# The second layer of a gated feed-forward kernel turned over: 26 products of weight block sums, read back from DRAM, with gated block sums of 512 tokens

## The chip, the core and the metric

The kernel runs on one core of one Trainium2 chip. A core has a matrix engine (TensorE; PE in the profile, with its weight loads as PEld), three engines for elementwise work (VectorE is DVE, ScalarE is ACT, GpSimd is POOL) and SyncE (SP), which here only starts DMA transfers. SBUF is the on-chip memory of 128 partitions, PSUM the small memory that TensorE writes its products to, DRAM the memory off the core. Each engine works through its own queue in order; an instruction that waits holds everything behind it in that queue. The metric is the time of one execution on the device in microseconds (us), lower is better. The kernel before has a median of 660.98 us in three runs (660.61 to 662.32).

## The reference

Two blocks follow each other. A retention block turns q, k and v (4 batches, 8 heads, 768 steps, 64 numbers each) into 3072 rows of 512, with a decaying state per head. A feed-forward block multiplies these rows by W_in, gates the result and multiplies by W_out:

```python
for t in range(S):
    state = gamma[None, :, None, None] * state + np.einsum('bhd,bhe->bhde', k[:, :, t], v[:, :, t])
    y[:, :, t] = scale * np.einsum('bhd,bhde->bhe', q[:, :, t], state)
x = y.transpose(0, 2, 1, 3).reshape(3072, 512)
h = x @ w_in                      # (512, 2048)
sp = np.maximum(h, 0.0) + np.log1p(np.exp(-np.abs(h)))
g = h * erf(sp)
return (g @ w_out).astype(np.float32)     # w_out (2048, 512)
```

Everything is computed in 32-bit floats. The two weights arrive as 8-byte floats, and the kernel takes them apart and rebuilds them as 4-byte floats on VectorE and ScalarE while they are loaded.

## The kernel before

Tokens come in pieces of 128, numbered j (24 of them). The first 512 tokens (j = 0 to 3) go through an opening stage, with their hidden values in four groups g = 0 to 3 of 512 and plain products; this stage also loads and converts the weights and ends at about 132 us. All later tokens go through a loop over g = 4 to 23 (`for g in range(G0 + 1, NG)`, with g = 4 written out ahead of it). Two successive g are the two halves, s = 0 and 1, of the 2048 hidden values of one chunk of 256 tokens.

The first layer of a g (`hidden_steps`, line 987) replaces 32 block products by the 26 of a fast scheme, in the table `STEPS`. Each step is one product of a sum of W_in blocks with a sum of x blocks, 128 columns wide and two matmuls long. The W_in sums are made once (`sum_in`, line 385), the 18 x sums per chunk (`x_sums`, line 969). A step's result lies in one of four PSUM banks (tiles `hp` and `r`), and is copied by ScalarE or added by VectorE (line 999, 18 additions a g) into up to two blocks of h. The bank is free for its next step only then.

After the last step come Softplus (line 859) and Erf (line 866) on ScalarE, and two multiplications by h on VectorE (`gated`, line 885).

The second layer (`project_part`, line 1070) uses the seven products of a 2 by 2 fast scheme (`PRODUCTS`) for each g: four matmuls of 128 x 128 by 256 columns each, the gated block held still and W_out (with its four sums T1 to T4) streamed, all from SBUF. Four gated sums a g come from VectorE (`g_sums`, line 1052). Three products of g - 1 are spread among the steps of g, four stand in a row at the end of g. The finished chunk is put together by VectorE (`put_part`) and written in two DMAs of 256 KB.

At the end of each g lies a visit of the recurrence (`sub_visit`): scores, state and values of the next 128 tokens in small matmuls of 64 x 64, masks (line 677), additions to the state (lines 819 and 839) and to the rows (line 834). `prepared` scales and transposes the next pieces of q and k on VectorE (five instructions a piece). `load(j)` starts the DMAs of a piece three ahead: one for k (line 208), 32 small ones of 16 KB for blocks of q and k (line 190, from `load_blocks`), one for v (line 218). All of them, and the writes of the output, are issued by SP.

The order of the work is written by hand: every engine gets its instructions in the order of the Python statements.

Of the kernel before, what the change touches and what calls it, by code (L numbers as in the profile page):

```python
# [25 lines left out]
FG = 4  # L26
# [9 lines left out]
OUT = {"11": 0, "12": 1, "21": 2, "22": 3, "T3": 1, "T1": 4, "T2": 5, "T4": 6}  # L36

PRODUCTS = {
    1: ("11", "11"), 2: ("12", "21"), 3: ("S4", "22"), 4: ("22", "T4"),
    5: ("S1", "T1"), 6: ("S2", "T2"), 7: ("S3", "T3"),  # L40
}

N_W, N_X = 26, 18
W_SUMS = (
# [83 lines left out]

OP = {"+": ALU.add, "-": ALU.subtract}
# [5 lines left out]
def kernel(  # L140
# [31 lines left out]
    act = ctx.enter_context(tc.tile_pool(name="act", bufs=2))  # L172
# [4 lines left out]


# [16 lines left out]
    def load(j):  # L195
        b, c = divmod(j, NC)
        if j == JPC - 1:

            x = act.tile([P, N], F32, name="e", bufs=1)
            KQ[j] = x[:, : 2 * d_model].rearrange("p (i h d) -> p i h d", i=2, h=H)  # L200
            V[j] = x[:, 2 * d_model : 3 * d_model].rearrange("p (h d) -> p h d", h=H)
        else:
            KQ[j] = loads.tile([P, 2, H, D], F32, name="kq")
            V[j] = loads.tile([P, H, D], F32, name="v")
# [21 lines left out]
    w_out_sb = const.tile([P, 2, 7, FG, DH], F32, name="w_out_sb")  # L226
# [5 lines left out]
    def w_out_of(ft):  # L232
        half, s, i = ft // (2 * FG), ft % (2 * FG) // FG, ft % FG
        return w_out_sb[:, s, 2 * half : 2 * half + 2, i, :]
# [4 lines left out]
    spare = [w_out_sb[:, s, 4:7].rearrange("p a b c -> p (a b c)") for s in range(2)]  # L239
# [4 lines left out]
    LO = slice(2 * CE + 2, 2 * CE + 2 + CE // 2)  # L244
    whole_powers = [later[:, i * CE : (i + 1) * CE].bitcast(U32) for i in range(2)]
    powers = [
        [x.bitcast(U16) for x in two] for two in (
            (spare[0][:, LO], spare[1][:, LO]),
            (later[:, : CE // 2], later[:, CE // 2 : CE]),
            (spare[1][:, : CE // 2], spare[1][:, CE // 2 : CE]),  # L250
        )
# [18 lines left out]
    def load_piece(n, *parts):  # L270
# [16 lines left out]
        else:  # L287
            for d in range(2):
                nc.sync.dma_start(
                    w.rearrange("p (d f c) -> p d f c", d=2, f=2)[:, d],  # L290
                    x[i * 2 * P : (i + 1) * 2 * P, d * words * DH : (d + 1) * words * DH].rearrange(
                        "(f p) c -> p f c", p=P
                    ),
                )

    def load_pieces_after(n):
        for later in range(n + 1, n_p):
            if place[later] == place[n]:
                load_piece(later)
                break  # L300

    def whole_conversion(n):
# [6 lines left out]
        for part, rows in parts:  # L309
            last = n > 0 or rows.start == 1  # L310
            words = spare[place[n]][:, : 2 * CE].bitcast(U32)
            if which == "in":
                f = slice(2 * P) if part is None else slice(part * P, (part + 1) * P)
                fb = 2 * half + at
                to = w_in_sb[:, s, 4 * fb : 4 * fb + 4, f].rearrange("p (h k) f -> p h k f", h=2)
            else:
                to = w_out_sb[:, s, 2 * half : 2 * half + 2, at * 2 : at * 2 + 2, :]
            words = words.rearrange("p (h a b w) -> p h a b w", h=2, a=2, w=2)
            power = whole_powers[n % 2].rearrange(
                "p (h q a b) -> p q h a b", q=1 if part is None else 2, h=2, a=2  # L320
# [28 lines left out]
    def shifted_conversion(n):  # L349
# [3 lines left out]
        words = spare[place[n]].bitcast(U32)[:, : 2 * CE].rearrange("p (h a b w) -> p h a b w", h=2, a=2, w=2)  # L353
        top = spare[place[n]].bitcast(U16)[:, 4 : 4 + 4 * CE].rearrange(
            "p (h a b w) -> p h a b w", h=2, a=2, w=4
# [4 lines left out]
        else:  # L360
            to = w_out_sb[:, s, 2 * half : 2 * half + 2, at * 2 : at * 2 + 2, :]
        up, down = (
            x.rearrange("p (h a b) -> p h a b", h=2, a=2) for x in powers[2 if n == n_p - 1 else n % 2]
# [24 lines left out]
    def sums(s):  # L388

        assert ("project", s) in done  # L390
        x = {name: w_out_sb[:, s, at] for name, at in OUT.items()}
        for to, a, b in (("T1", "12", "11"), ("T2", "22", "T1"), ("T3", "22", "12"), ("T4", "21", "T2")):
            nc.scalar.activation(x[to], x[b], AF.Copy, scale=-1.0)
            nc.gpsimd.dma_start(x[to], x[a], accum_op=ALU.add)
            done.add((to, s))
            yield

# [14 lines left out]
    def later_sums():  # L412
        for s in range(2):
            yield from sums(s)

    weight_steps = weights()
    last_steps = later_sums()
# [9 lines left out]
    def need(*what):  # L427
        nonlocal room
        while what not in done:
            cost = next(weight_steps, None)  # L430
            if cost is None:
                next(last_steps)
            room -= cost or 0
# [4 lines left out]
    ident = const.tile([P, P], F32, name="ident")  # L438
# [18 lines left out]
    causal = const.tile([P, C], F32, name="causal")  # L457
# [17 lines left out]
    adds_of = {JPC: range(2), JPC + 1: range(1), JPC + 2: range(1)}  # L475
    assert (JPC + 2) % NC == 0 and NC > 1

# [25 lines left out]
    kq_b = const.tile([P, NC, 2, HP, 4], F32, name="kq_b")  # L503
    by_b = const.tile([P, 2, HP], F32, name="by_b")

    def load_block_scales(g):
        nc.gpsimd.tensor_copy(idle_out, HS[g][:, N - 1 :])
        for s, d in itertools.product(range(2), range(2)):
            part = slice((2 * s + d) * 32, (2 * s + d + 1) * 32)
            for u in range(HP):  # L510
                nc.gpsimd.dma_start(
                    kq_b[part, 0, 0, u],
# [4 lines left out]
    def block_scales():  # L517
        nc.vector.reciprocal(by_b[:, 0], by_b[:, 1])
        nc.vector.reciprocal(kq_b[:, 0, 1], kq_b[:, 0, 0])
        nc.vector.tensor_scalar(kq_b[:, 0, 1], kq_b[:, 0, 1], unscale, None, op0=ALU.mult)  # L520
        for c in range(1, NC):
            nc.gpsimd.tensor_tensor(
                kq_b[:, c], kq_b[:, c - 1], by_b[:, :, :, None].to_broadcast([P, 2, HP, 4]),
                op=ALU.mult,
# [50 lines left out]
    def prepared(j):  # L575

        if j >= NJ:
            return
        nc.vector.tensor_tensor(
            KQ[j][:, 0], KQ[j][:, 0],  # L580
            kq_s[:, j % NC, 0, :, None].to_broadcast([P, H, D]), op=ALU.mult,
        )
        yield
        blocks = (KB[j], KQ[j][:, 1].rearrange("p h d -> p (h d)"))
        for i, x in enumerate(blocks):
            x = x.rearrange("p (u a d) -> p u a d", u=HP, d=32)
# [801 lines left out]
```

## Time and profile before

| what | value |
|---|---|
| median of three runs | 660.98 us (660.61 to 662.32) |
| span of the profiled execution, first to last instruction | 659.9 us |
| PE busy | 654.1 us, 99% |
| DVE, ACT, POOL busy | 504.4, 289.6 and 21.5 us |
| one g in the loop (from 183.17 to 286.85 us are four) | 25.92 us |
| DVE busy in those 103.68 us | 78.86 us |
| granted TensorE clock | 1.00 throughout |
| bytes read and written in DRAM | 40.39 and 6.29 MB |

The profiled execution gives no time of its own beside its span; the median run is 1.1 us above that span. In the rows of groups, a line of the kernel, an engine and an operation are followed by the tiles written and read, the shape and the number of records; then busy time in all, the mean duration of one in nanoseconds, and the idle time of the engine ahead of them. A 32-bit matmul makes two records. Durations of neighbours overlap, so that a row of n instructions in the timeline takes less than n times the mean; in the timeline the first number is the start and the second the length of the whole row.

### The profile page before, as it was taken

To read this page: it belongs to the slowest core of one execution; us is meant where nothing else is said; L and a number is where in the kernel's file an instruction comes from. 1 tells how busy PE (TensorE), PEld (TensorE's weight loads), DVE (VectorE), ACT (ScalarE), POOL (GpSimd) and SP (SyncE) were. 2 spreads that over 40 slices of the span, in tenths; PEclk is the share of its full clock that TensorE was granted. 3 is DMA by queue.
4 is the path that set the end of the run, shared out by engine and by line. 5 is a ranking of instruction groups with operands and counts; after the bars stand their busy time and mean duration, and the time that the engine had idled before them with its cause. 6 is when DMAs were issued, how large, how long until landed. Compare 5 with 4: busy or idle time off the path is not lost.

```text
span 659.9 us, 15375 instructions
## 1 busy us (share of the span) xinstructions
PE 654.1 (99%) x6240; PEld 556.8 (84%) x6240; DVE 504.4 (76%) x1112; ACT 289.6 (44%) x410; POOL 21.5 (3%) x49
## 2 busy tenths in 40 slices
PE   8999999999999999999999999999999999999998
PEld 7744444487999999999999999999999999999997
DVE  5999879988886886787778678677787788476464
ACT  3468584527625334244254253342432542543440
POOL 1000061101100000000000000000000000000000
PEclk9999999999999999999999999999999999999999
DMA  9999972555843321222222322222231210000000
GB/s 190 222 236 220 211 246 43 107 100 120 165 77 59 79 47 35 68 44 48 68 46 45 73 39 50 60 52 42 38 80 34 45 55 1 1 35 1 1 32 33
DMA packets 157511, 51.90 MB, mean 79 GB/s; under 512 B 141312, under 2 KB 147840, under 8 KB 157440
## 3 DMA queue, kind: packets, MB, share of 16 engines
q1 hardware_dynamic: 155328, 46.71, 33.3%
q0 software_dynamic: 1696, 4.21, 3.4%
q8 instruction: 49, 0.80, 0.5%
q14 instruction: 22, 0.18, 0.1%
q10 hardware_dynamic: 416, 0.01, 0.0%
HBM read 40.39 MB, written 6.29 MB: 71 GB/s over the span
## 4 chain that ended last, share of the span: by engine, by line
PE 95%; DVE 3%; DMA 1%; SPq 0%; issue 0%; ACT 0%
PE o L1070 37%; PE hp L987 23%; PE r L987 12%; PE hp L896 8%; PE o L932 6%; PE r L778 2%; PE hp L670 1%; PE o L814 1%; DMA kq<-in_k_dram 1%; DVE w_in_sb L385 1%; PE r L599 1%; PE o L646 1%; PE r L793 1%; DVE xs L969 1%; PE hp L793 1%; PE r L566 1%
## 5 line engine op out<-in xcount | busy, mean ns | idle before, releaser
L987 PE MATMUL hp<-xs,w_in_sb 128*128 128x128 f32 x1040 | 145.6, 275 | 0.0
L1070 PE MATMUL o<-w_out_sb,h 128*128 128x256 f32 (+1 forms) x640 | 142.7, 380 | 0.0
L987 PEld LDWEIGHTS hp<-xs,w_in_sb 128*128 128x128 f32 x1040 | 135.2, 192 | 4.0 <-issue 0.7
L999 DVE TENSOR_TENSOR h<-h,hp 128x256 f32<-128x256 f32 x200 | 82.1, 419 | 73.6 <-PE hp L987 68.5
L1070 PEld LDWEIGHTS o<-w_out_sb,h 128*128 128x128 f32 x640 | 119.5, 190 | 16.6
L1070 PE MATMUL o<-w_out_sb,e 128*128 128x256 f32 x480 | 113.5, 379 | 0.0
L859 ACT ACTIVATE e<-h 128x2048 f32<-128x2048 f32 x22 | 42.0, 1910 | 120.6 <-DVE h L999 120.6
L1070 PEld LDWEIGHTS o<-w_out_sb,e 128*128 128x128 f32 x480 | 86.8, 190 | 9.4
L999 DVE TENSOR_TENSOR h<-h,r 128x256 f32<-128x256 f32 x160 | 59.9, 416 | 21.7 <-PE r L987 20.6
L1001 ACT COPY h<-hp 128x256 f32<-128x256 f32 x40 | 14.9, 373 | 134.6 <-PE hp L987 106.5
L987 PE MATMUL r<-xs,w_in_sb 128*128 128x128 f32 x480 | 66.7, 275 | 0.4 <-DVE am L677 0.4
L987 PEld LDWEIGHTS r<-xs,w_in_sb 128*128 128x128 f32 x480 | 60.0, 192 | 0.6 <-PE hp L987 0.6
L896 PE MATMUL hp<-xT,w_in_sb 128*128 128x512 f32 (+2 forms) x144 | 56.6, 548 | 0.0
L885 DVE TENSOR_TENSOR e<-h,e 128x1024 f32<-128x1024 f32 x42 | 49.3, 1213 | 8.0 <-ACT e L866 8.0
L987 PE MATMUL hp<-xT,w_in_sb 128*128 128x128 f32 x320 | 48.9, 275 | 0.0
L896 PEld LDWEIGHTS hp<-xT,w_in_sb 128*128 128x128 f32 x144 | 25.7, 190 | 27.2 <-issue 24.6
L987 PEld LDWEIGHTS hp<-xT,w_in_sb 128*128 128x128 f32 x320 | 43.6, 192 | 1.5 <-issue 0.5
L866 ACT ACTIVATE e<-e 128x2048 f32<-128x2048 f32 (+1 forms) x23 | 42.1, 1836 | 0.2
L1003 ACT ACTIVATE h<-hp 128x256 f32<-128x256 f32 x60 | 23.0, 384 | 31.1 <-PE hp L987 29.8
L987 PE MATMUL r<-xT,w_in_sb 128*128 128x128 f32 x240 | 33.3, 275 | 0.0
L866 ACT ACT_TABLE_LOAD x24 | 30.8, 1283 | 0.4
L987 PEld LDWEIGHTS r<-xT,w_in_sb 128*128 128x128 f32 x240 | 30.0, 192 | 0.0
(176 smaller groups left out, 778.6 us busy)
## 6 DMA issues: line engine op xcount, KB each, us to landing
w_out_sb<-in_moe_w_out_dram SPq DMA_DIRECT2D x14, 512.0 KB, 7.8
kq<-in_k_dram SPq DMA_DIRECT2D x23, 256.0 KB, 4.0
v<-in_v_dram SPq DMA_DIRECT2D x23, 256.0 KB, 3.4
out_dram<-r SPq DMA_DIRECT2D x23, 256.0 KB, 2.7
kq<-in_q_dram SPq DMA_DIRECT2D x288, 16.0 KB, 1.8
kb<-in_k_dram SPq DMA_DIRECT2D x288, 16.0 KB, 1.7
w_in_sb<-in_moe_w_in_dram SPq DMA_DIRECT2D x8, 512.0 KB, 13.2
w_out_sb<-w_out_sb POOLq DMA_DIRECT2D x8, 512.0 KB, 5.1
```

Of the source, the lines that this page charges most:

```text
L778: nc.tensor.matmul(pp[r][col * D : (col + 1) * D, u % 2, t], x[own, u, :], QT[j][own, u, t], start=first(r, col), stop=True, skip_group_ch ...
L793: nc.tensor.matmul(other[a][own, u % 2, D:] if crossed else pp[a][own, u % 2, t], V[j][t, 2 * u + r, :], AM[j][t, r, u, :D], start=crossed ...
L859: nc.scalar.activation(E[g], HS[g], AF.Softplus)
L866: nc.scalar.activation(E[g][:, half], E[g][:, half], AF.Erf)
L885: nc.vector.tensor_tensor(E[g][:, half], HS[g][:, half], E[g][:, half], op=ALU.mult)
L896: nc.tensor.matmul(HP_[ft][:, t], w_in_of(ft, kk), XC[0][:, kk, t], start=(kk == 0), stop=(kk == n_k - 1),)
L932: nc.tensor.matmul(O[0][tt].rearrange("p (d c) -> p d c", d=2), E[g][:, u * TCH + tt * P : u * TCH + (tt + 1) * P], w_out_of(ft), start=(f ...
L987: nc.tensor.matmul(to[:, u, :], w_in_sb[:, s, w, u * P : (u + 1) * P], XS[m](x), start=first and u == 0, stop=True, skip_group_check=True,)
L999: nc.vector.tensor_tensor(h, h, of, op=ALU.add if plus else ALU.subtract)
L1001: nc.scalar.copy(h, of)
L1003: nc.scalar.activation(h, of, AF.Copy, scale=-1.0)
L1070: nc.tensor.matmul(O[m][i][:, half, at], G[g][a][:, u * P : (u + 1) * P], w_out_sb[:, s, OUT[b], u, at], start=i not in started, stop=(s = ...
```

## The change

The gated blocks of two chunks (512 tokens, four successive g, called M here) are multiplied together. The seven products of each g are given up for the 26 of the first layer's own table `STEPS`, used once for M: the weight side is one of 26 sums of W_out blocks (128 x 512 numbers, 256 KB), held still, and the gated side is one of the h blocks or of 18 sums of them, 1024 columns in SBUF, streamed as four matmuls of 256 columns. The result is the transposed output.

- The 26 sums of W_out are made once during g = 4 to 7 (`operand_sums`), two of three on POOL, and written to DRAM. Each product reads its sum back through a ring of four buffers, `WS`: the load for a product is issued by SP right behind the product four places earlier.
- The 18 sums of gated blocks for each M are made in place, every second one on POOL, every third in the last M.
- Results are collected in SBUF (`R`: 8 copies by ScalarE, 18 additions by VectorE for each M), transposed in blocks of 32 by VectorE and written with four DMAs for each of eight blocks (`put`).
- The 26 products of an M begin at the end of its fourth g and are spread over the next four: four in the first layer of a g and two or three at its end, behind `load(j + 3)`. The last M's 26 stand at the end, in the order `LAST_STEPS`.
- Erf and the gate of g move into the first layer of g + 1 (behind its steps 10, 18 and 19).
- The recurrence's visit is split into `begin`, `begun` and `results`; ten of the 18 x sums go to POOL for all chunks but the first.
- At g = 4 the remaining W_in sums come ahead of the first step, and the four projections of the first tokens' last group move into g = 4 and g = 5. h, gated blocks and weights share one tile (`arena`). W_out is loaded in other pieces of the same size, and its T sums by accumulating DMAs are gone.

```diff
-PRODUCTS = {
-    1: ("11", "11"), 2: ("12", "21"), 3: ("S4", "22"), 4: ("22", "T4"),
-    5: ("S1", "T1"), 6: ("S2", "T2"), 7: ("S3", "T3"),
-}
+S_STEPS = (
+    ("sum", 0, (1, 0), (1, 1), "-"), ("sum", 5, (1, 0), (0, 1), "-"), 0, 3, 1, 5,
+    ("sum", 7, (3, 1), 0, "-"), ("sum", 8, (1, 0), 7, "+"), 7,
+    ("sum", 4, (3, 0), (2, 0), "-"), ("sum", 10, 7, 4, "-"), 4, 8, 12,
+    ("sum", 1, (0, 0), (0, 1), "-"), 14, 15, ("sum", 6, (2, 0), 1, "+"), 11,
+    ("sum", 9, (0, 1), 6, "+"), 20, ("sum", 12, (2, 1), 6, "-"), ("sum", 13, (3, 1), 12, "-"), 9, 13, 16,
+    ("sum", 14, 9, 13, "-"), 19, ("sum", 15, (3, 0), 13, "-"), 25, ("sum", 11, (3, 0), 7, "-"), 2,
+    ("sum", 2, 1, 5, "-"), 6, 10, ("sum", 16, 2, 15, "+"), 17, 21, ("sum", 17, 5, 16, "+"), 18,
+    ("sum", 3, 5, 0, "-"), 22, 23, 24,
+)
...
+    def load_operand():
+        nonlocal loaded
+        if loaded < len(W_ORDER):
+            nc.sync.dma_start(
+                WS[:, loaded % 4].rearrange("p u c -> p (u c)"), w_out_d[W_ORDER[loaded]]
+            )
+        loaded += 1
...
+    def second_layer(M):
...
+        def sums():
...
+                engine = nc.gpsimd if turn % (3 if order is LAST_STEPS else 2) == 0 else nc.vector
+                engine.tensor_tensor(block(blocks[to]), *ins, op=OP[sign])
...
+        while at < len(order):
+            w, x, bank, first, reads = STEPS[order[at]]
...
+            for u in range(FG):
                 nc.tensor.matmul(
+                    to, WS[:, used % 4, u], rhs[:, u * 2 * P : (u + 1) * 2 * P],
+                    start=first and u == 0, stop=True, skip_group_check=True,
                 )
+            used += 1
+            load_operand()
+            for o, plus in reads:
+                r = R[:, o]
+                if o in written:
+                    nc.vector.tensor_tensor(r, r, to, op=ALU.add if plus else ALU.subtract)
...
+            for o, _ in reads:
+                if reads_left[o] == 0:
+                    put(M, o)
             yield
+            sums()
...
+        nc.vector.transpose(ro, R[:, o])
+        for i in range(4):
+            nc.sync.dma_start(
+                out[t0 : t0 + 2 * P, c * P + i * 32 : c * P + (i + 1) * 32].rearrange("(b y) x -> y b x", y=32),
+                ro[i * 32 : (i + 1) * 32].rearrange("y (b x) -> y b x", x=32),
+            )
...
+    for g in range(G0, NG):
+        i = g - G0
+        here = i % 4
...
+        for n, _ in enumerate(first_layer(g), start=1):
+            if i < 2 and n in (8, 18):
+                tt = 2 * i + (n == 18)
+                project(G0 - 1, tt)
+                put_first(tt)
+            if n % 3 == 0 and 6 <= 26 * i + n <= 103:
+                next(operands, None)
+            if i == 0 and n % 2 == 0:
+                sum_in(1, min(len(W_SUMS), n // 2 * 3))
+            if n in (4, 9, 14, 20):
+                next(next_chunk, None)
+            if n in ((5, 20, 22, 24) if here == 0 else (5, 11, 17, 23)):
+                product()
+            if i and n == 10:
+                late_erf(g - 1)
+            if i and n in (18, 19):
+                gate(g - 1, n - 18)
         all_of(next_chunk)
+        if i == 3:
+            all_of(operands)
+            free.extend(range(8, NB_))
+            for _ in range(4):
+                load_operand()
+        if here == 3:
+            product(26)
+            steps_done = 0
+            products = second_layer(macro_of(g))
+            next(products)
         nc.scalar.activation(idle, idle, AF.Softplus)
         if more:
+            results(j)
+            if j + 1 < NJ:
+                begin(j + 1)
+        softplus(g)
...
+            x_sums(m, X_FIRST, nc.vector)
+            x_sums(m, X_REST, nc.gpsimd)
         if more:
+            if j + 1 < NJ:
+                begun(j + 1)
             if j + 3 < NJ:
                 load(j + 3)
             j += 1
+        if g + 1 < NG:
+            product(3 if here in (2, 3) else 2)
+
+    g = NG - 1
+    late_erf(g, 2)
+    for half in range(2):
+        gate(g, half)
+    for _ in products:
+        pass
```

## The prediction

> **What bounds the kernel now.** I read the busy times first, then the chain that ended last, the groups, the engines' timelines of one g in the loop, and SP's timeline.
>
> ```profile
> PE 654.1 (99%) x6240; PEld 556.8 (84%) x6240; DVE 504.4 (76%) x1112; ACT 289.6 (44%) x410; POOL 21.5 (3%) x49
> ...
> PE 95%; DVE 3%; DMA 1%; SPq 0%; issue 0%; ACT 0%
> ...
> L1070 PE MATMUL o<-w_out_sb,h 128*128 128x256 f32 (+1 forms) x640 | 142.7, 380 | 0.0
> ...
> L1070 PE MATMUL o<-w_out_sb,e 128*128 128x256 f32 x480 | 113.5, 379 | 0.0
> ```
>
> TensorE sets the time from end to end; the last two rows are the second layer of the later tokens, 1120 records. The chain gives their prices in rows that stand back to back:
>
> ```profile
> 267.35 1.73 PE o L1070 x8
> 269.08 1.34 PE hp L987 x12
> ```
>
> 1.73 / 8 = 0.216 us for a record of 256 columns, so 1.73 for a product (four matmuls, eight records); 1.34 / 12 = 0.112 for 128 columns, so 0.45 for a first-layer step of four records and 11.65 for the 26 steps. A g of 25.92 us is 11.65 + 7 x 1.73 + 2.1 for the recurrence (251.90 to 253.99).
>
> ```profile
> 234.03 2.35 DVE L885 TENSOR_TENSOR e<-h,e 128x1024 f32<-128x1024 f32 x2
> ...
> 240.32 1.40 DVE L999 TENSOR_TENSOR h<-h,r 128x256 f32<-128x256 f32 x4
> ```
>
> VectorE in a queue: 1.13 us for 1024 columns (the second starts that much after the first), 0.33 for 256 and, from the starts of other neighbours, 0.6 for 512 and 0.2 for 128.
>
> ```profile
> 252.91 0.38 SPq L208 DMA_DIRECT2D kq<-in_k_dram  x1
> 253.35 9.11 SPq L190 DMA_DIRECT2D kq<-in_q_dram  x16
> 262.56 8.82 SPq L190 DMA_DIRECT2D kb<-in_k_dram  x16
> 271.48 0.39 SPq L218 DMA_DIRECT2D v<-in_v_dram  x1
> ```
>
> This row carries the forecast. One `load(j)` holds SP's queue from 252.91 to 271.87: 19.0 us of a g of 25.92. Other blocks take 17.5 (from 201.07), 18.2 and 18.0 (from 511.63). Today nobody waits for what stands behind it: only the output.
>
> **The change part by part, against the profiled execution's 659.9 us.**
>
> *Products.* 20 g x 7 = 140 products become 5 x 26 = 130, of the same shape: 10 x 1.73 = **-17.3**. First layer and recurrence keep their matmuls.
>
> *Opening of the loop, g = 4 to 7: +16.* These g have almost no second layer, because a product needs the gates of earlier chunks and M is complete only after g = 7; the work moves to the end, where it is PE's alone. What PE then waits for, each time:
> - Ahead of g = 4 VectorE does, from 121.59: 10 weight sums 3.9, 18 x sums 4.1, two gates 2.35, masks and state 1.5, so step 1 comes at 133.5 and not 132.4, and with no projection (3.44, 127.8 to 131.4) done: 4.5.
> - In g = 4 all 30 sums of the other half run on VectorE (0.394 each from 5.52 / 14: 11.8), with 18 additions (about 6.2), five instructions of 512 (3.0) and two operand sums (1.2): 22.2 against PE's 11.65 + 2 x 3.44 = 18.5; before, this g already lost 0.7: 3.0.
> - The boundary after g = 5: results 0.7, copies 0.6, additions 0.5, eight x sums 1.8, masks 0.75, state 0.8 = 5.1 against 2.1 of PE's own, with no products to fill it: 3.0.
> - g = 6: behind step 17 VectorE has two gates (2.3), nine additions (3.0), 0.6 + 0.6, against PE's 4.0: 2.4 late, and a boundary of 3.7 against 2.1: 4.0 less what slack I allow, 3.5. g = 7 the same 2.4 late, its boundary partly under products: 2.
>
> *SP's queue: +58.* The loads of weight sums for a g's last products stand behind `load(j + 3)`, and are the operands of the products four places later. The ring is full again only then. From the end of the n = 23 product: SP issues its load (0.4), `load(j + 3)` (18.2, the mean of the four), then the next, which waits for nothing more; landing 2.7 (out, 256 KB in 2 KB rows). So the n = 17 product of the next g starts 21.3 later. PE alone would be there after 1.3 + 2.1 + 2 x 1.73 + 17 x 0.45 + 2 x 1.73 = 18.0. Behind it come 1.73, six steps 2.7, 1.73: the cycle is 27.5. In the g with three products at its end (`here` 2 to 3) the n = 11 product is the one that waits: 31.9. From `here` 3 to 0 the output's DMAs (four at 0.45 behind a transpose) hold SP 2.5 and the n = 20 product waits: 30.4, to n = 24; from there 29.6. Four g: 119.4, against 4 x 13.75 + 26 x 1.73 = 100.0. From n = 24 of g = 8 to n = 23 of g = 19 (the last `load`) that is 2 x 119.4 + 89 = 327.8, against 285 steps, 11 visits and 71 products = 273.6: 54; and 4 at the first wait in g = 8.
>
> The ends: issues at the median of 0.43 with gaps of 0.04 make a block of 16.1, and a landing of 1.7 (out, 128 KB) makes it 34 less over 11 cycles; the block of 22.6 (from 154.83, at a DMA share of 0.81) makes it 48 more. I take the middle because the loop's own share (0.29) lies near those four blocks.
>
> *VectorE.* Four g hold 72 + 18 additions, 8 gates, 9 sums of 1024, 20 instructions of 512, 8 transposes (no row; as 256 columns, 0.33; 0.7, the 512 row, at most), 23 small ones and 16 x sums: 73 us of queue, where 78.9 are busy now. So not the bound, and its lateness inside a g (1 to 3 us, below) lies under SP's waits while there are `load`s; g = 20 to 23 pay 3.
>
> *POOL.* No row has 128 x 1024 there. 128 x 32 takes 326 ns and 128 x 8 takes 285: 2.0 us by that slope, 5.4 us if the fastest of the small ones (203) is the base. Nine an M and ten x sums each second g fit in 100 us either way (28 to 65). I take 2.0, since the mean is nearer than the minimum. [...]
>
> *Loads of weights at the start.* W_out pieces land in runs of 1 KB, not 2 KB. W_in's first pieces already do, at 222 GB/s (slice 2), beside 211 to 246 in the slices behind: nothing, and if its 8 MB came 10% slower, 4 us at most.
>
> *The end.* The last M has 26 products with no other work (45 us, in the sum). PE does two, then waits for Softplus, a table (1.28), Erf and the copy behind them in ACT's queue: 2.4, then 0.5 and 1.3 for sums behind an addition: +4. The output behind the last product is like now.
>
> **Sum:** 659.9 - 17.3 + 16 + 58 + 3 + 4 = 723.6; the median lies 1.1 above the span: **725 us**.
>
> **Rivals.**
> - *SP keeps ahead, VectorE's order decides: 690.* Then each M loses what in-order queues cost: after `here` 0 the second end product shares a bank with the first, whose copy stands behind Softplus (1.4); after 1, gates and sums put VectorE 1.5 behind and the addition that frees the bank stands behind x sums and masks (1.9); after 2, three products in one bank (1.8); 0.3. 6.9 x 3.8 = 26: 659.9 - 17.3 + 16 + 26 + 4 + 1.1. For it: landing and issue might be quicker with SP's stream less dense. Chance 0.25.
> - *POOL and VectorE exclude each other: 750.* If a sum on POOL stops VectorE's, eight x sums wait 0.49 each at nine boundaries (35), and a third of 43 sums of 2.0 falls where PE waits (29): 690 + 64, put at 750. Against it: five POOL sums ran from 110.90 to 112.85 beside VectorE's weight sums, which took 414 to 464 ns, median 424. Those were small. Chance 0.10. [...]
> - *Faster: 656.* SP's block must fall to 14.9 us or less, so that 0.4 + block + 2.7 is within PE's 18.0; its fastest issues (311 ns, 12.1 a block) would do it. With VectorE's slack covering its order and half the opening's waits: 659.9 - 17.3 + 8 + 4 + 1.1 = 655.7. All blocks seen are 2.6 or more above that point. Chance 0.09.
> - That the products are not fewer is excluded by the order of the matmuls: 520 of 256 columns for 560.
>
> **Numbers.** The forecast's own case has 0.54, and 0.02 remains for no change. A run of this kernel tells about 0.3%, 2 us. Faster 0.09, same 0.02, slower 0.89. The range leaves out the faster rival and the farther parts of both sides: 672 (the second case with a third less loss at the opening and half the bank waits) to 765 (the block at 22.6, a sixth of its 48 covered).
>
> **What would show it.** PE's idle from g = 8 to 19 before products, released by DMA of the weight sums, 2 to 6 us each, at n = 17, 11 and 20; SP without a gap there; a g of 27 to 32 us. In g = 4 to 7 PE 75 to 85% busy, with releases by VectorE. If those idle times are released by VectorE or ScalarE, the first rival holds; if its instructions with two SBUF inputs grow by 0.5 us or more beside POOL, the second. Wrong altogether: PE at 97% or more in g = 8 to 19.

## The result, and the profile after

The changed kernel takes **833.3 us** in the median of four runs (831.7 to 835.3), the kernel before 660.8 beside it (660.6 to 662.3): a ratio of 1.259, interval 1.255 to 1.263. The forecast was 725 with a range of 672 to 765. The sign was right, the size too small by 108 us. The profiled execution has a span of 830.5 us.

From the page of the changed kernel: busy times, the granted TensorE clock in 40 slices, and the chain that ended last.

```profile
PE 693.9 (84%) x6152; PEld 575.9 (69%) x6152; DVE 541.9 (65%) x1066; ACT 296.4 (36%) x443; POOL 188.4 (23%) x193
...
PEclk9999999897998979999999999999998999999899
...
PE 48%; DVE 29%; DMA 7%; issue 5%; ACT 5%; SPq 3%; POOL 2%; DVEq 0%; ACTq 0%
```

PE issues 88 matmul records fewer and is yet busy for 39.8 us more (654.1 before). The clock row has 7s and 8s, where before it was 9 throughout. And PE is no longer the whole chain: 48%, with 29% for VectorE, where the row before read 95% and 3%.

The waits of PE (line, what ended the wait; total us, times, longest us):

```profile
PE hp L993 <- DVE arena L1007: 58.6, 45, 5.1
PE o L1096 <- DMA arena<-w_out_d: 25.9, 9, 4.7
PE o L1096 <- DVE arena L1105: 17.1, 12, 3.1
PE hp L993 <- DVE state L792: 6.0, 2, 4.3
PE hp L993 <- POOL arena L1147: 3.5, 1, 3.5
PE o L1096 <- DVE arena L1084: 3.4, 2, 2.8
```

L993 is a first-layer step, L1007 VectorE's addition that reads the step's bank and so frees it; L1096 is a second-layer product, L1105 the addition that frees its bank, L1084 a block sum, L792 the recurrence's state, L1147 a W_out sum on POOL. The largest item is not SP's queue (second row) but the first layer waiting for banks that VectorE has not yet read.

From the start and end records of PE and the records of its clock I made this table (not a view): each stage of the loop, how long it took, how long PE was idle, and what PE lost to stretches at half the granted clock (half of its busy time in them). The last two columns are kernels of the experiments.

| stage (g of the first layer) | before: us | after: us / idle / half clock | loads cut apart | and banks spaced |
|---|---|---|---|---|
| 4 to 7 | 102.6 | 115.1 / 27.9 / 11.1 | 119.9 / 30.1 / 13.8 | 119.4 / 31.2 / 11.9 |
| 8 to 11 | 103.4 | 140.1 / 24.8 / 11.7 | 124.6 / 18.5 / 1.7 | 117.7 / 13.0 / 1.0 |
| 12 to 15 | 103.7 | 133.9 / 23.6 / 6.1 | 127.4 / 19.2 / 3.4 | 119.6 / 12.4 / 3.5 |
| 16 to 19 | 103.4 | 138.2 / 26.5 / 7.7 | 124.7 / 18.6 / 1.7 | 118.3 / 12.4 / 2.4 |
| 20 to 23 | 92.3 | 110.4 / 16.1 / 0.0 | 113.7 / 16.0 / 3.4 | 103.2 / 9.5 / 0.8 |
| behind the last first layer | 19.1 | 54.4 / 5.9 / 2.4 | 54.3 / 6.1 / 2.0 | 54.8 / 5.9 / 2.9 |

Over the whole span: 129.1 us idle between PE's records (1.3 before) and 38.9 lost to half clock (none before). 659.9 - 17.3 for the products + 127.8 + 38.9 is 809.3; 21.2 remain to 830.5. Some 13 of them are what a break costs in the busy time itself: a record of 128 columns lasts 0.275 us where the next one starts 0.112 behind it, and a break shows the difference, 0.163, in 82 more places than before. The other 8 I can't place.

Two places show the two kinds of wait. First SP's queue, in the timeline of the changed kernel (start, us, engine and line, transfer):

```profile
239.48 0.38 SPq L243 DMA_DIRECT2D kq<-in_k_dram  x1
239.91 9.96 SPq L225 DMA_DIRECT2D kq<-in_q_dram  x16
249.91 8.72 SPq L225 DMA_DIRECT2D kb<-in_k_dram  x16
258.73 0.39 SPq L253 DMA_DIRECT2D v<-in_v_dram  x1
259.22 14.44 SPq L1044 DMA_DIRECT2D arena<-w_out_d  x7
```

The block of loads holds SP for 19.6 us, and the first weight sum behind it is issued at 259.22. PE had stopped at 259.13 and went on at 263.39.

Second, VectorE's order, in the g that starts at 280.4 (the last bracket is idle time and what ended it):

```profile
287.49 0.71 DVE L1007 TENSOR_TENSOR arena<-arena,r 128x256 f32<-128x256 f32 x2
288.52 1.91 ACT L1026 ACTIVATE e_even<-e_even 128x2048 f32<-128x2048 f32 x1
...
290.33 0.36 ACT L1109 ACTIVATE arena<-o 128x256 f32<-128x256 f32 x1
290.73 0.42 DVE L1105 TENSOR_TENSOR arena<-arena,o 128x256 f32<-128x256 f32 x1 [2.53 <-ACT arena L1109]
291.07 0.75 DVE L1007 TENSOR_TENSOR arena<-arena,r 128x256 f32<-128x256 f32 x2
291.73 0.96 DVE L1007 TENSOR_TENSOR arena<-arena,hp 128x256 f32<-128x256 f32 x2
292.20 0.71 PE L993 MATMUL hp<-xs,w_in_sb 128*128 128x128 f32 x4 [1.90 <-DVE arena L1007]
```

A product's first copy (L1109) stands on ScalarE behind the Erf (L1026). VectorE's next instruction is the addition onto that copy (L1105), so VectorE itself stands idle for 2.53 us, with four first-layer additions queued behind it, and PE idles for 1.90 with its banks full. VectorE is 65% busy and still holds PE up. Such a stop of VectorE behind a third engine makes up four pauses, at this place in g = 9, 13, 17 and 21. In most others VectorE works: by the start and end records PE waited 78.3 us for an addition of VectorE (17.2 of them in g = 4 to 7), and VectorE was busy for 74.2 of these, with the gates, sums and additions that stand ahead in its queue.

### The profile page after: what moved, and what is told of

Same layout as the page of the kernel before. It is cut to its first block, busy times and chain, and to the rows that moved or that the text cites. A ratio compares the mean times of both kernels' runs of the same rounds, so it can differ in the third digit from the quotient of the medians.

```text
span 830.5 us, 16001 instructions
## 1 busy us (share of the span) xinstructions
PE 693.9 (84%) x6152; PEld 575.9 (69%) x6152; DVE 541.9 (65%) x1066; ACT 296.4 (36%) x443; POOL 188.4 (23%) x193
## 4 chain that ended last, share of the span: by engine, by line
PE 48%; DVE 29%; DMA 7%; issue 5%; ACT 5%; SPq 3%; POOL 2%; DVEq 0%; ACTq 0%
PE o L1096 22%; PE hp L993 13%; DVE arena L1007 6%; PE r L993 6%; DVE arena L1030 5%; DMA arena<-w_out_d 4%; DVE w_in_sb L421 2%; SPq L225 2%; DVE xs L975 2%; DVE arena L1105 2%; DVE arena L1084 2%; DMA w_in_sb<-in_moe_w_in_dram 2%; PE r L816 1%; POOL arena L1147 1%; PE o L930 1%
## 5 line engine op out<-in xcount | busy, mean ns | idle before, releaser
L1096 PE MATMUL o<-arena 128*128 128x256 f32 x1040 | 262.7, 403 | 55.3 <-DMA arena<-w_out_d 25.9
L1096 PEld LDWEIGHTS o<-arena 128*128 128x128 f32 x1040 | 200.8, 201 | 92.0 <-DVE arena L1105 21.9
L993 PE MATMUL hp<-xs,w_in_sb 128*128 128x128 f32 x1040 | 159.3, 289 | 62.2 <-DVE arena L1007 58.6
L993 PEld LDWEIGHTS hp<-xs,w_in_sb 128*128 128x128 f32 x1040 | 140.4, 201 | 74.1 <-DVE arena L1007 67.5
L1084 POOL TENSOR_TENSOR arena<-arena 128x1024 f32<-128x1024 f32 x42 | 102.2, 2438 | 300.8 <-DVE arena L1084 198.8
L1007 DVE TENSOR_TENSOR arena<-arena,hp 128x256 f32<-128x256 f32 x200 | 81.3, 415 | 81.8 <-PE hp L993 79.3
L1007 DVE TENSOR_TENSOR arena<-arena,r 128x256 f32<-128x256 f32 x160 | 60.5, 409 | 60.5 <-PE r L993 59.2
L1105 DVE TENSOR_TENSOR arena<-arena,o 128x256 f32<-128x256 f32 x90 | 37.1, 418 | 92.8 <-PE o L1096 82.2
L993 PE MATMUL r<-xs,w_in_sb 128*128 128x128 f32 x480 | 72.6, 286 | 0.0
L993 PEld LDWEIGHTS r<-xs,w_in_sb 128*128 128x128 f32 x480 | 67.1, 203 | 1.8
L1084 DVE TENSOR_TENSOR arena<-arena 128x1024 f32<-128x1024 f32 x48 | 61.9, 1291 | 5.4 <-PE o L1096 5.4
L993 PE MATMUL hp<-xT,w_in_sb 128*128 128x128 f32 x320 | 52.8, 292 | 10.5 <-DVE state L792 6.0
L1030 DVE TENSOR_TENSOR arena<-arena,e_even 128x1024 f32<-128x1024 f32 x40 | 59.2, 1483 | 1.8 <-ACT e_even L1026 1.8
L993 PEld LDWEIGHTS hp<-xT,w_in_sb 128*128 128x128 f32 x320 | 48.2, 206 | 12.7 <-issue 11.0
L1147 POOL TENSOR_TENSOR arena<-arena 128x512 f32<-128x512 f32 x20 | 30.6, 1542 | 78.8 <-DVE arena L1147 67.1
L1026 ACT ACTIVATE e_even<-e_even 128x2048 f32<-128x2048 f32 (+1 forms) x21 | 38.3, 1828 | 0.2
L993 PE MATMUL r<-xT,w_in_sb 128*128 128x128 f32 x240 | 34.7, 283 | 0.0
```

The costliest lines, as they stand in the source:

```text
L993: nc.tensor.matmul(to[:, u, :], w_in_sb[:, s, w, u * P : (u + 1) * P], x_at(x), start=first and u == 0, stop=True, skip_group_check=True,)
L1007: nc.vector.tensor_tensor(h, h, of, op=ALU.add if plus else ALU.subtract)
L1026: nc.scalar.activation(e_even[:, at], e_even[:, at], AF.Erf)
L1030: nc.vector.tensor_tensor(x, x, e_even[:, half * BL : (half + 1) * BL], op=ALU.mult)
L1084: engine.tensor_tensor(block(blocks[to]), *ins, op=OP[sign])
L1096: nc.tensor.matmul(to, WS[:, used % 4, u], rhs[:, u * 2 * P : (u + 1) * 2 * P], start=first and u == 0, stop=True, skip_group_check=True,)
```

## The experiments

My theory after the result: three costs add up. SP's queue (Q) is one, the order on VectorE (O) the larger, and PE's pauses bring stretches at half clock (H). The forecast said Q, with 3 us for O. In the kernels below the first layer's lines stand 17 or 18 lines later than in the changed kernel (L1010 for L993, L1024 for L1007, L1113 for L1096, L1122 for L1105, L1101 for L1084, L1047 for the gate's L1030), if loads are cut apart; the lines of products and block sums one more where POOL's sums are short.

**Loads cut apart.** The 34 transfers of `load(j + 3)` are issued two at a time in the next g's first layer, so that a weight sum stands behind two of them at most.

```diff
         for n, _ in enumerate(first_layer(g), start=1):
...
+            next(loading, None)
+            next(loading, None)
...
-                load(j + 3)
+                loading = load_steps(j + 3)
```

> The changed kernel with load(j + 3) cut into its 34 DMAs, two behind each step of the next g's first layer, so that SP reaches the loads of the weight sums at once; nothing else moves. Queue theory (the prediction's main term): PE's 25.9 us of waits for the weight sums and the half-clock time behind each go, so 833 falls to 775 to 795 and PE <- DMA waits are under 5 us. Order theory (VectorE's lateness decides, SP only stands in its shadow): over 815.

808.2 us (806.9 to 809.5), ratio to before 1.223 (1.218 to 1.228). PE's waits in this kernel:

```profile
PE hp L1010 <- DVE arena L1024: 61.4, 49, 5.1
PE o L1113 <- DVE arena L1122: 17.5, 13, 3.0
```

The weight sums fall from 25.9 us of waiting to 1.9; the additions stay as they were. The queue was worth 25 us, not 58, and these 25 are not the waits alone: PE's idle time falls by 15.1 us (129.1 to 114.0) and its loss to half clock by 12.9 (38.9 to 26.0).

**No read-back.** Only the first four weight sums are read from DRAM.

```diff
-        if loaded < len(W_ORDER):
+        if loaded < 4:
```

> The changed kernel with only the first four weight sums read back; the other 126 loads are left out and the products use what lies in the ring, so part of the operands is not the computation's. Queue theory: about the time of the kernel with the spread loads, within 10 us. If that one gains and this one gains 15 us more, the stream of 34 MB itself costs time beside its place in the queue.

802.2 us, 6 below the kernel with the loads cut apart. So the stream of 126 transfers costs 6 us at most once it is not queued behind the blocks.

**No sums on POOL**, in the changed kernel and with the loads cut apart.

```diff
-                engine = nc.gpsimd if turn % (3 if order is LAST_STEPS else 2) == 0 else nc.vector
+                engine = nc.vector
```

(the same for the W_out sums and the x sums)

> The changed kernel with every sum that it gives to POOL put on VectorE (42 of 1024 columns, 20 of 512, 90 of 128: about 77 us of VectorE's queue at undisturbed durations). Port theory (VectorE and POOL stop each other): gates fall from 1483 to about 1220 ns, and the time falls by 20 us or more in spite of the added work. Order theory (VectorE is late because it has too much in a row): gates fall too, but the time rises to 840 to 860.

> The two edits together. If queue and port are two separate causes, the gains add: about 750. If VectorE's order is what is left once SP is out of the way, the added sums cost more here than alone: over 800.

853.8 and 827.0 us: 20.5 and 18.8 slower than the same kernels with POOL. (The port in these two expectations was my guess at a cause; no run here shows one, only how long the instructions of the two engines take beside each other.) PE's wait for the additions of products goes from 17.1 to 32.1. More work in VectorE's queue makes PE wait more: for O. POOL's help outweighs what it does to VectorE. Both runs lie in the range of the order theory (840 to 860, and over 800).

**POOL's block sums short**, with the loads cut apart.

```diff
-                engine.tensor_tensor(block(blocks[to]), *ins, op=OP[sign])
+                w_ = 8 if engine is nc.gpsimd else BL
+                engine.tensor_tensor(block(blocks[to])[:, :w_], *(x[:, :w_] for x in ins), op=OP[sign])
```

> The loads cut apart, and only POOL's share of the block sums cut to 8 of 1024 columns (so these sums are not computed); VectorE's are full. With all sums short 774.2 us, with none short 808.2. Theory P (POOL and VectorE hold each other up: the gates take 1483 ns beside POOL's sums and 1213 before, POOL's sum 2438): 780 to 790 and the gates back under 1300 ns. Theory V (VectorE's own sums and what stands behind them): 795 to 806, the gates no faster in the sum of time that PE sees.

796.0 us, 12.2 less: the time lies in theory V's range, the gates under 1300 ns are theory P's sign. The groups of this kernel (mean ns of one after the busy time), a block sum and the gate:

```profile
L1102 DVE TENSOR_TENSOR arena<-arena 128x1024 f32<-128x1024 f32 x48 | 58.3, 1215 | 4.0 <-PE o L1114 4.0
L1047 DVE TENSOR_TENSOR arena<-arena,e_even 128x1024 f32<-128x1024 f32 x40 | 50.6, 1267 | 1.8 <-ACT e_even L1043 1.8
```

With POOL's sums at full length these rows read 1361 and 1472 ns, and the gate 1213 before. These means are misleading: it is not every instruction that slows down by a fifth. At full length 76 of the 88 take at most 1.23 us; the other twelve take 1.6 to 3.3, each beside a sum on POOL (in the changed kernel 77, and eleven of 1.6 to 3.3). With POOL's block sums short only four gates are longer, beside other sums of POOL. One such place in g = 11 of the changed kernel (g = 15 and 19 have the same):

```profile
371.36 2.35 POOL L1084 TENSOR_TENSOR arena<-arena 128x1024 f32<-128x1024 f32 x1 [13.53 <-DVE arena L1030]
371.47 3.32 DVE L1030 TENSOR_TENSOR arena<-arena,e_even 128x1024 f32<-128x1024 f32 x1
...
377.56 0.71 PE L993 MATMUL hp<-xs,w_in_sb 128*128 128x128 f32 x4 [3.07 <-DVE arena L1007]
```

The gate starts 0.11 us behind POOL's sum and ends 1.08 behind its end; as it takes 1.22 elsewhere, hardly any of its work can have been done before that sum ended. The pause of PE that follows, 3.07 us in g = 11, 15 and 19, is 0.96 with POOL's sums short, 2.11 less, which is what the gate lost. So the two engines do hold each other up where they meet: the gate takes 3.32 us for 1.22 here (its mean is 1216 ns in the kernel without sums on POOL, 1483 with them), and at 777.07 POOL's sum takes 3.17 for 2.35 beside a block sum of VectorE that began at 776.81. But few instructions meet: with the loads cut apart the two groups lose 17 us of VectorE's time, 15 of them to POOL's block sums, and without the length of these the kernel gains 12.

**All block sums short**, VectorE's too.

```diff
-                engine.tensor_tensor(block(blocks[to]), *ins, op=OP[sign])
+                engine.tensor_tensor(block(blocks[to])[:, :8], *(x[:, :8] for x in ins), op=OP[sign])
```

> The loads already cut apart (the kernel that took 808.2 us), and in it each of the 18 sums of gated block sums per four g only 8 of 1024 columns wide, on VectorE and POOL alike; the order of the work, the copies and all additions stay. What it multiplies is then no longer the sums, only their length in time is gone. Theory A (the order on VectorE and POOL: the sums stand ahead of the first layer's additions and of the banks' additions): five times 18 sums of 1.2 to 2.4 us shrink, PE's pauses in the later g fall from about 19 us to under 8 us per four g and the time to 720 to 760. Theory B (the sums lie beside other work; the pauses come from the copies on ScalarE and from the place of the gates): 790 to 808. PE alone would need about 100 us per four g, or some 663 in all.

774.2 us (770.5 to 777.8), between the two theories. 34 us go, of which POOL's share was 12. The waits for the additions of products stay (17.5 to 17.1 us): these are not a matter of how long the sums take. Those of the first layer fall from 61.4 to 43.8, so a part of them is the length of the sums that stand ahead of the additions.

**Products spaced over the banks.** With the loads cut apart, the list of the last M, in which neighbouring products write other banks, serves for every M, and the weight sums are read in that order. (With it two of three block sums go to VectorE rather than one of two.)

```diff
-        order = LAST_STEPS if M == macro_of(NG - 1) else S_STEPS
+        order = LAST_STEPS
```

> The loads cut apart (the kernel that took 808.2 us), and the products of every four g in the order of the last ones, in which products that stand together write different banks; the places of the products in the g, the Erf and the gates stay. Theory A1 (waits for the addition that frees a bank, 17.1 us released by the additions of products, plus the half clock behind the 3.05 us ones): 785 to 795, these waits under 6 us. Theory A2 (this order needs its sums earlier and makes the products wait for them instead): 800 to 820, with releases by the block sums in their place.

773.4 us, 35 less: more than expected, and as much as by leaving out the length of every sum, though VectorE now does 12 block sums more. PE's waits:

```profile
PE hp L1010 <- DVE arena L1024: 52.0, 49, 5.1
PE hp L1010 <- DVE state L809: 6.5, 4, 4.3
PE o L1113 <- DMA arena<-w_out_d: 6.1, 3, 2.3
PE o L1113 <- DVE arena L1101: 5.1, 4, 2.8
```

The waits for L1122 fall from 17.5 to 0.6, and with them the pause of 3.05 us per M behind such an addition. The other long one, 3.07, falls to 0.96 as it did with POOL's sums short: here POOL has 30 block sums for 42, and the gate no longer meets one at that place. O holds; this edit moves the sums too, so how much of the 35 is the banks alone is not separated.

**Erf later**, behind step 12 instead of 10, with the loads cut apart.

```diff
-            if i and n == 10:
+            if i and n == 12:
                 late_erf(g - 1)
```

> The loads cut apart, and the Erf of the g before issued after step 12 of the first layer instead of step 10. Theory A1 (the pause of 1.9 us in the g after the first of a group comes from ScalarE's copy of a first-layer result that stands behind the Erf): this pause is gone or shorter, 800 to 806. Theory A2 (the gates come later with it, and the block sums behind them): the pauses near steps 24 and 25 (1.64) grow by as much, 806 to 820.

795.9 us (793.8 to 797.9), 12 less and below the expected range. The pause of 1.90 us falls to 0.58, and the pauses of 1.64 near steps 24 and 25 do not grow. Four such pauses make 5.3 of the 12 us; 3.9 more are half clock (26.0 to 22.1), and 1.7 lie ahead of the first step of g = 4, where the edit changes nothing.

**The three together**, with a third of the weight sums of g = 4 on POOL.

```diff
+        for at, (to, a, b, sign) in enumerate(W_SUMS[in_sums[s] : upto]):
+            engine = nc.gpsimd if s == 1 and at % 3 == 1 else nc.vector
```

> Loads cut apart, products ordered over the banks in every four g, the Erf after step 12, and a third of the 26 weight sums of the other half in g = 4 on POOL. The parts add up if the waits are apart from each other: the banks 15, the Erf 4, the opening 5, so about 784. Theory A2 (one wait taken away uncovers the next): 795 or more. Neither comes near 661: the opening alone stands 46 us above PE's own work of 69 in g = 4 to 7.

773.7 us, the same as the spaced products alone and below both forecasts, because the spaced products had gained 35 and not 15. In the spaced order the pause at the Erf's place is 0.87 already where it was 1.90, so most of what the later Erf gained is not there to gain again; and g = 4 to 7 takes 119.5 us as before (119.4), for PE's idle time there falls by 2.8 us and the half clock grows by 3.1. What the edits gain one by one does not add up.

**The old boundary.** Loads cut apart, Erf and gates at the end of their own g as in the kernel before, spaced products.

```diff
-            if i and n == 10:
-                late_erf(g - 1)
-            if i and n in (18, 19):
-                gate(g - 1, n - 18)
...
+        late_erf(g, 2 if g == NG - 1 else 1)
+        if g + 1 < NG:
+            product(2)
+        for half in range(2):
+            gate(g, half)
+            if g + 1 < NG:
+                product()
```

> The loads cut apart, and the order of the later tokens turned back towards that of before: the Erf and the gates at the end of their own g, behind masks and x sums, four products at the end of each g and two or three in the first layer, and in every four g the product order of the last ones, in which neighbouring products use other banks. Theory A (the order is what costs): 730 to 780, below the 808.2 of the kernel with the loads cut apart alone. Theory B (the sums and the additions are too much for VectorE wherever they stand): 790 to 830.

787.3 us, in neither theory's clear range: 21 better than the loads cut apart alone, 14 worse than the spaced products with the late Erf. PE now waits 31.2 us for block sums that VectorE makes (up to 6.9 at a time) and 13.8 for POOL's: at the end of an M's fourth g they stand in the queues behind masks, state and x sums. Half of the 40 gates now meet a sum on POOL and take 1.4 to 3.4 us. Once, behind g = 7, PE stands for 12.9 us ahead of the first product. But g = 8 to 19 are 3.5 to 5 us slower per M as well, so the old boundary as a whole is no better than the new one.

**The clock.** In the kernel before, four or eight extra VectorE instructions of 0.69 us (a maximum of a block with itself) stand in each g ahead of the last four products, whose operand they write; PE has no other work than before.

```diff
         gate_erf(g)
+        for _ in range(4):
+            x = G[g - 1]["S1"]
+            nc.vector.tensor_tensor(x, x, x, op=ALU.max)
         for p in (5, 6, 7, 3):
```

> The kernel before, with four extra VectorE instructions of 0.6 us (512 columns each, result unchanged) in each of 19 g, between the Erf's gates and the last four additions of products: 2.4 us per g, 45.6 us of VectorE in all, no more work for PE. Theory A (a pause costs its length): at most 660.8 + 45.6 = 706, and less by what slack VectorE has. Theory C (a PE pause of about 3 us also brings a stretch of 3.4 us at half the granted clock, 1.7 us lost): up to 32 us above the pauses, and low-clock stretches in the records after each pause.

> The same with eight of them, 4.8 us per g, 91.2 us of VectorE in all. Theory A: at most 752, and the difference to the run with four no more than 45.6. Theory C: the difference to the run with four is above 45.6, PE's own busy time rises by 20 to 32 us although it has the same work, and stretches at half clock follow the pauses; in the kernel before there is one of 0.6 us.

838.9 and 906.7 us. I had the pauses wrong: writing the products' operand makes PE wait for all that VectorE does in between, 7.4 us a g and not 2.4. From the profile of the run with four, its busy times and clock, then PE's largest wait; and the busy times with eight:

```profile
PE 688.3 (82%) x6240; PEld 580.5 (70%) x6240; DVE 554.9 (67%) x1188; ACT 289.7 (35%) x410; POOL 21.9 (3%) x49
...
PEclk9999999979897997989889798888979889898999
```

```profile
PE o L1070 <- DVE h L1312: 140.1, 19, 8.6
```

```profile
PE 700.7 (78%) x6240; PEld 589.3 (65%) x6240; DVE 607.5 (67%) x1264; ACT 289.5 (32%) x410; POOL 21.8 (2%) x49
```

The size of the pause is measured, so the question is answered all the same: with the same 6240 records PE is busy for 34.2 us more with four (688.3 against 654.1) and 46.6 more with eight. Its busy time inside half-clock stretches is 68.4 and 93.2 us, twice that. H holds for its cost; whether the pauses cause the half clock, or VectorE's extra work does, was open. So the next two fill the pauses with matmuls that nobody uses, and change nothing else:

```diff
+        fill = ps_r.tile([P, HP, C], F32, name="r").rearrange("p u t -> p (u t)")
+        for _ in range(17):
+            nc.tensor.matmul(
+                fill[:, : 2 * P], w_in_sb[:, 0, 0, :P], w_in_sb[:, 0, 1, :], start=True, stop=True,
+            )
```

> The kernel before with four extra VectorE instructions in each of 19 g (838.9 us, PE pauses of 7.4 to 8.6 us), and in each pause eight matmuls of 256 columns into a bank that nobody reads: 8 x 0.43 = 3.5 us of additional PE work. Theory W (the granted clock halves after a stretch of 3.41 us in which PE was busy for less than about 0.44 of it): pauses of 4 to 5 us are left, each still empties more than 0.56 of such a stretch, the half clock stays: 826 to 842. Theory N (half clock comes from something else in these kernels, VectorE's work or the place in the g): the same, 830 to 842.

> The same with 17 matmuls, 17 x 0.43 = 7.35 us of additional PE work in each pause: 0 to 1.2 us of pause are left, and the last three pauses (3.3 to 4.5 us) are overfilled by some 11 us in all. Theory W: no stretch is under 0.44 busy any more, the half clock is gone and with it 34 us, so 838.9 - 34 + 11 = 816, 806 to 824, although PE does 140 us of work that nobody uses. Theory N: 839 to 850, with the stretches at half clock unchanged.

830.7 us with 8, 818.9 with 17. Busy times and clock with 17:

```profile
PE 796.8 (98%) x6886; PEld 679.4 (83%) x6886; DVE 555.1 (68%) x1188; ACT 289.7 (35%) x410; POOL 21.5 (3%) x49
...
PEclk9999999999999999999999999999999999999999
```

PE does some 140 us of unused matmuls, VectorE the same as with four (555.1 against 554.9), and the kernel is 20 us faster: the half clock is gone. The pauses caused it.

No version came near the kernel before: the best, 773.4, is still 17% slower (1.168, interval 1.159 to 1.178). In it PE is idle for 88.8 us, 31.2 of them in g = 4 to 7, and loses 22.5 to half clock; no run here takes the waits of the opening away.

## Why the prediction was wrong

By its own steps, against the places where the 108 us lie: the first layer of g = 8 starts at 247.4 where the forecast's terms put it at about 220 (27 us), from there to g = 20 it takes 412.3 where they give 358 (54), and from there to the last matmul it is 22 longer than they left for it. The other 5 are in the last output and in the distance of the median from the profiled span.

- **Products, -17.3: right.** 80 records of 256 columns fewer, at 0.216 from start to start in both kernels.
- **Opening, +16: too small.** The four g take 115.1 us where PE's own work by the forecast is 68.8 and 5.2 for the products at the end of g = 7. The idle time alone is 27.9, and 3.3 ahead of g = 4. The places named were there: 3.34 ahead of g = 4 (4.5 forecast), 5.10 in g = 4 (3.0), 4.28 at the boundary after g = 5 (3.0), 6.4 in g = 6 and behind it (3.5), 5.1 in g = 7 (2). Not named were 1.45 and 1.23 more about g = 4, and 1.17 and 3.08 in g = 5. The step failed at its method, a few places worked out by hand. The sum would have warned: the windows of these four g give VectorE's busy time as 26.64 + 18.84 + 17.41 + 20.69 = 83.6 us, and the same four of before 83.1, while the forecast's opening came to 68.8 + 11.5 = 80.3. Its 11.1 us of half clock were not in the step at all. The products taken out of the opening moved to the end, as forecast: there PE needs 54.4 us where it needed 19.1.
- **SP's queue, +58: mechanism right, size wrong.** The block took 17 to 20 us as forecast and the weight sums landed behind it, and PE waited where the step said, at n = 20, 17 and 11, for 2.2 to 4.7 us at a time. But it named four waits per M, and the one at n = 17 of the third g did not come; PE waited 25.9 us in all and the cut gained 25. The step let PE run at its own pace between the waits; by the waits of the table above VectorE slowed PE there, so that SP was back in time more often, which is argued and not shown by a run.
- **VectorE, "lies under SP's waits", +3: this step failed, and it is the largest.** Its 73 us of queue in 100 were right as a count (83 busy in the 137 of a real M), and so was "not the bound". But being late for a bank needs no full engine, only something long ahead of the addition in its queue. From g = 8 on PE waited 61.1 us for additions; these waits added to SP's instead of hiding under them, and with SP's gone they stayed. VectorE was busy for 57 of them with its own gates, sums and additions; in four pauses it had stood behind ScalarE, and in four of 2.4 to 3.1 us a gate had stood behind POOL. In g = 8 to 19 alone the forecast's 58 us stand against 112 (412.3 less 300 of PE's own): 25 of waits for weight sums, 50 of other waits, nearly all for VectorE, and 25.5 of half clock; most of the last 12 is the broken pipeline. The first rival had the mechanism of these waits, with its places (the end product whose bank is freed behind masks and x sums: 3.05 measured, 1.9 forecast), and 26 us for it. It failed as a forecast because it was made to exclude the queue.
- **POOL at 2.0 us: 2.44 measured** (x42, 102.2 us; 2.35 in the median).
- **POOL and VectorE excluding each other (second rival, 750): seen, price too high.** On average the gate grew from 1213 to 1483 ns, below the 0.5 that I named as the sign; but 32 of the 40 did not grow at all, and of the eight that did, all beside POOL, six grew by 0.7 to 2.1. The rival let every x sum at the boundaries and a third of the block sums wait (64 us); 11 of the 88 gates and block sums were held up. Without POOL's length the kernel gains 12 us; without POOL it loses 20. In the gate above the wait is plain, 3.32 us where it takes 1.22; what in the chip makes it wait is not shown.
- **The end, +4: right within 2.** Pauses of 2.78, 0.47, 2.0 and 0.65.
- **Loads at the start, 0: right.** The first step of g = 4 comes at 132.2, against 132.4.
- **Left out altogether: the half clock, 38.9 us**, and some 13 for the broken pipeline. The kernel before has 1.3 us of idle time in all, so nothing in its trace shows this; the forecast priced each wait at its length.

## What to carry to other kernels

When a change takes work away from the engine that was always busy, don't ask only whether the other engines have enough time in total: walk each in-order queue and find what stands ahead of the instruction that frees the next bank: long work of the same engine, an instruction that waits for a third engine, or one that another engine holds up. Read durations one by one where engines may hinder each other: a gate's mean that is a fifth higher (1483 ns for 1213) was here eight instructions of 40, four of which took two microseconds more. Waits on different queues are to be added until a trace shows that one covers the other. And look at what follows a pause of TensorE: with the loads cut apart, 2.46 us of idle TensorE within one stretch of 3.41 us (from 310.40) were followed by 3.41 us at half clock, 1.7 us more by half its busy time in them; a pause of 3.07 us that lay in two such stretches was not.

## What the runs showed of the hardware

I had not expected the half clock to go with PE's pauses as closely as it does. In the clock records of the changed kernel the granted clock is 1.0 or 0.5, and each of its 39 changes lies a whole multiple of 3.413 us behind the start of the records, through all the pauses. I took PE's busy share in each such stretch of 3.41 us from the one in which g = 4 starts to the last matmul. In the 19 stretches behind which the clock fell to half, PE was busy for 0.00 to 0.44 of the time; of the 157 behind which it stayed full, one had 0.44 and all others 0.46 or more. Once at half, it came back behind 19 stretches in which PE was busy for 0.81 or more, and stayed at half behind eight with 0.17 to 0.79. So in this kernel it mattered where a pause fell in these stretches. The windows of the kernel with the loads cut apart show it on two pauses of nearly one length, 3.05 us behind g = 9 (from 309.81) and 3.07 in g = 11 (from 366.62); columns are the stretch, its length, busy time of PE, PEld, DVE, ACT and POOL, the granted clock, DMA share and GB/s:

```profile
310.40:313.81 3.41, 0.95 (x4) 0.87 (x5) 2.33 (x7) 0.00 (x0) 2.88 (x7) 1.00 0.23 77
313.81:317.22 3.41, 3.41 (x13) 2.98 (x12) 1.41 (x2) 0.37 (x1) 3.41 (x4) 0.50 0.17 29
317.22:320.64 3.42, 3.42 (x25) 3.21 (x24) 0.52 (x2) 1.26 (x4) 2.31 (x1) 1.00 0.69 159
365.01:368.42 3.41, 1.61 (x10) 1.29 (x8) 3.41 (x5) 0.00 (x0) 0.84 (x1) 1.00 0.49 106
368.42:371.83 3.41, 2.14 (x78) 2.02 (x82) 2.55 (x7) 0.00 (x0) 0.00 (x0) 1.00 0.23 41
```

The first pause lies in one stretch, which is left with 0.95 us of PE (0.28), and the next stretch runs at 0.50. The second is split over two stretches, with 1.61 (0.47) and 2.14 us (0.63) of PE, and the clock stays at 1.00. By these figures of the changed kernel, as an estimate, a pause under 1.84 us (3.41 less 0.46 of it) would not have lowered the clock by itself, and one of 4 us would leave some stretch at 0.41 or less, where the clock fell each time. Parts of two pauses in one stretch also went before a fall: in the one from 767.29 us PE stood for 1.58 and 0.68 us and was busy for 1.16 (0.34), and the next, from 770.70, ran at 0.50. In g = 4 to 7 of that kernel PE was idle for 27.9 of 115.1 us, and the clock fell six times, twice for two stretches.
